# The first gate input loaded and scanned in two halves, and the early shares of the DMA engines in a planner set anew

## The chip, the cores and the metric

One core of a Trainium2 chip runs the kernel. The metric is device time in microseconds of one execution, as the median of several. The profile of one execution lists every instruction with its engine, its line, its start and what released it. The engines are TensorE (PE; its weight loads are listed as PEld), VectorE (DVE), ScalarE (ACT), GpSimd (POOL) and SyncE (SP). SP issues loads, stores and transposing transfers, POOL issues the weights' transfers, and 16 DMA engines move all of them.

## The reference

A gated linear attention over 4 batches, 8 heads, 768 steps and 48 channels, and behind it a gated feed-forward block over the 3072 tokens:

```python
f = 1.0 / (1.0 + np.exp(-f_logit))
for t in range(S):
    state = f[:, :, t, :, None] * state + np.einsum('bhd,bhe->bhde', k[:, :, t], v[:, :, t])
    y[:, :, t] = np.einsum('bhd,bhde->bhe', q[:, :, t], state)
x = np.ascontiguousarray(y.transpose(0, 2, 1, 3)).reshape(B * S, H * D)
gate = np.maximum(x @ w_gate, 0.0)      # 384 -> 1536
val = x @ w_val
out = (gate * val) @ w_out              # 1536 -> 384
```

## The kernel before, in words

**Tiling.** The sequence is cut into six chunks of 128 steps. The first four chunks are worked in pairs: a *unit* (d, b) is pair d (chunks 2d and 2d + 1) of batch b, so there are eight units; units (0, 0) to (0, 3) are called unit 0, 1, 2, 3 here. Chunks 4 and 5 are worked chunk by chunk (`attention_front`, `attention`). The 512 tokens of one chunk over four batches go through the feed-forward block together.

**One unit** (`attention_unit`). Four loads bring f, k, q and v (`load_unit`, 384 KB each, rows of 384 bytes). They are called f0, k0, q0, v0 for unit 0, and so on. ACT turns f into log gates (Exp at L587, Ln at L588, into `bneg`). PE sums them along the sequence with triangular matrices (the scan, L595 and L596: two PSUM banks, two products of 384 columns each). ACT takes exponentials of the sums (L600, L602) and of the totals (L626, into `decu`). POOL multiplies k by them (L604) and DVE multiplies q (L607), into `hats`. In pair 0, PE transposes the `hats` (L638) and DVE or ACT copies them to `qkT` (L646, L647); in later pairs a transposing transfer does it, issued by SP (L554, called a turn). PE multiplies q by k (scores, L677), DVE masks them into `ptm` (L682), POOL copies v into `vpad` (L613), PE forms the update of the state (L659), DVE and POOL update it (L569, L572, L574), and PE forms the outputs inside and across the halves (L708, L693). ACT or DVE copies them to `xT` (L724).

**Feed-forward.** For each of twelve blocks j of 128 hidden channels PE makes a gate bank and a value bank (L894, three products each, a *pass*), ACT takes the relu (L900) and DVE multiplies (L904, into `gT`). In the first group of 512 tokens, blocks 0 to 5 are done for two batches at a time (passes of 256 columns, twelve pairs of passes in all), blocks 6 to 11 for four at once (512 columns). Then PE multiplies `gT` by the output weights (L917), ACT copies (L927, into `osb`) and SP stores (L931).

**Weights.** POOL issues them in three parts each: wg0 and wv0 cover blocks 0 to 2, wg1 and wv1 blocks 3 to 5, wg2 and wv2 blocks 6 to 11, and wo0 to wo2 the output weights. Each waits for a load, as the list `first` says: `wg0@k0` is issued once k0 has landed, in POOL's queue between POOL's other work.

**What sets the order.** Every engine runs a fixed queue. A planner (class `Plan`) writes it when the kernel is built: a list schedule with a cost for each operation, in which the operation that can start first goes first, and due times of transfers from class `Rings`. `Rings` holds the loads' queue (`hw`) and the weights' queue (`sw`). While weights are moving, loads get a share of the engines and take longer by that much (`through`):

```python
SHARE, AHEAD, LAND = 0.16, 1500, 0.65
...
self.sw_free = begin + work / 0.87
```

The plan is made four times over, each time with the weights' stretches of the last. On the chip an operation waits for semaphores alone; due times decide only where it stands in its queue. Behind the plan, gaps of PE before 24 us are filled with products of zeros that keep PE active (`warm`, L976): so many as the planned gap divided by a cost for each.

**The first scan's place.** ACT's queue begins with Exp and Ln of f0, which wait for f0's landing; PE's queue has zeros before the first scan. POOL's queue has wg0's issue before the first k products.

Of the kernel before, what the change touches and what calls it, by code (L numbers as in the profile page):

```python
# [5 lines left out]
AF = mybir.ActivationFunctionType  # L6
# [38 lines left out]
class Rings:  # L45


    SHARE, AHEAD, LAND = 0.16, 1500, 0.65

    def __init__(self, busy):  # L50
        self.busy = busy
# [6 lines left out]
    def through(self, t, work):  # L58
        for a, b in self.busy:
            if b <= t:  # L60
                continue
            if t < a:
                if work <= a - t:
                    return t + work
                work -= a - t
                t = a
            if work <= (b - t) * self.SHARE:
                return t + work / self.SHARE
            work -= (b - t) * self.SHARE
            t = b  # L70
        return t + work

# [25 lines left out]

    def sw(self, at, work):
        begin = max(at, self.sw_free)  # L100
        self.sw_free = begin + work / 0.87
        self.made.append((begin, self.sw_free))
        return self.sw_free + self.LAND


class Plan:
# [9 lines left out]
    def add(self, eng, emit, reads=(), writes=(), occ=0.5, lat=0.2, prio=0, opens=(), after=(), follows=()):  # L116
        op = Op(eng, emit, list(reads), list(writes), occ, lat, prio, opens, after, follows)
        op.idx = len(self.ops)
        self.ops.append(op)
        return op  # L120
# [190 lines left out]
def bass_hgrn2_outer__then__ffn_reglu_kernel(  # L311
# [11 lines left out]
    pe_hats = {0}  # L323
    x_way = {4: "xbar", 5: "xbar"}
    flight = (4, 2)
    first = "f0 k0 q0 f1 v0 k1 q1 v1 wg0@k0 wv0@v0 wg1@k1 wv1@q1 f2 wg2@v1 wv2@wg1 k2 wo0@wv1 wo1@wg2 q2 v2 wo2@v2 f3 k3 q3 v3".split()
    B, H, S, D = q.shape
    C = 128
    NC = S // C
    HD = H * D  # L330
# [14 lines left out]
    bneg = sb("bneg", [128, NB, 2, H, 64], BF16)  # L345
# [30 lines left out]
    upto = sb("upto", [128, C], BF16)  # L376
    below = sb("below", [128, C], BF16)
# [10 lines left out]
    add = pl.add  # L388
    gp, ve, sc, te, sy = nc.gpsimd, nc.vector, nc.scalar, nc.tensor, nc.sync
# [5 lines left out]
    PE_L = 0.17  # L395

    def act_t(n):
        return dict(occ=max(0.1, n * 0.00097), lat=0.3)
# [55 lines left out]
    def dma(op, slot, flow, n=1, descs=0, ring="hw"):  # L454

        if slot not in slots:
            slots[slot] = [nc.alloc_semaphore(f"d_{slot}"), 0]
        slots[slot][1] += 16 * n
        op.sem, op.goal = slots[slot]
        op.flow, op.descs, op.ring = flow, descs, ring  # L460

    srcs = {"f": f_logit, "k": k, "q": q, "v": v}

    def slot_of(n, c, pr):
        return (2 * c + pr) % NL[n]

    def in_keys(n, c, b0, b1):
        return [f"{n}{slot_of(n, c, b // 2)}_{b % 2}" for b in range(b0, b1)]

    def load_unit(n, d, b, after=()):  # L470
        t = ld[n]
        row = NL[n] * 2 * HD
        c, pr = 2 * d + b // 2, b % 2
        src = bass.AP(tensor=srcs[n].tensor, offset=b * H * S * D + 2 * d * C * D, ap=[[2 * D, 128], [S * D, H], [1, 2 * D]])
        dst = bass.AP(tensor=t, offset=slot_of(n, c, pr) * 2 * HD, ap=[[row, 128], [2 * D, H], [1, 2 * D]])
        last = tails.get("load")
        op = add("SP", lambda: sy.dma_start(dst, src), [], in_keys(n, c, 2 * pr, 2 * pr + 2), occ=0.5, lat=1.13,
                 prio=d * 200 + b * 10, after=after, follows=[last] if last else [])
        tails["load"] = op
        dma(op, f"{n}{slot_of(n, c, pr)}", 1.79 if n == "f" and d + b == 0 else 1.215, 1, 1024)  # L480
        return op

    def load(n, c, b0, b1, after=()):
# [18 lines left out]
    def load_w(nm, s, after):  # L502
        j0, j1 = WB[nm][s:s + 2]
        if nm == "wo":
            src = bass.AP(tensor=w_out.tensor, offset=j0 * 128 * DM, ap=[[DM, 128], [128 * DM, j1 - j0], [1, DM]])
            dst = wo[:, j0:j1, :]
        else:
            src = bass.AP(tensor=wsrc[nm].tensor, offset=j0 * 128, ap=[[DFF, 128], [128 * DFF, NK], [1, (j1 - j0) * 128]])
            dst = (wg if nm == "wg" else wv)[:, :, j0 * 128:j1 * 128]
        last = tails.get("load_w")  # L510
        op = add("POOL", lambda: gp.dma_start(dst, src), [], [f"{nm}{s}"], occ=0.8, lat=2.05, prio=0 if nm != "wo" and s < 1 else 20, after=after,
                 follows=[last] if last else [])
        tails["load_w"] = op
        dma(op, f"{nm}{s}", 2.5 if nm == "wo" else 0.53 + 0.44 * (j1 - j0), ring="sw")
        return op

    loads, done = [], {}
    for item in first:
        item, _, behind = item.partition("@")
        need = [done[behind]] if behind else []  # L520
        if item[0] == "w":
            op = load_w(item[:2], int(item[2:]), need)
        else:
            op = load_unit(item[0], 0, int(item[1:]), need)
            loads.append(op)
        done[item] = op

    def chain(line, *args, **kw):

        last = tails.get(line)  # L530
        tails[line] = add(*args, follows=[last] if last else [], **kw)
        return tails[line]
# [44 lines left out]
    def attention_unit(d, b):  # L577
        w0 = 8 * d + 2 * b
        late = d > 0 or b > 1
        P = w0 * 10 if late else (0, 6)[b]  # L580
        c0, pr = 2 * d + b // 2, b % 2
        raw = {n: ld[n][:, slot_of(n, c0, pr), :, :, :].rearrange("p b h d -> p (b h d)") for n in "fkqv"}
        by_i = {n: raw[n].rearrange("p (h i d) -> p i h d", h=H, i=2) for n in "fkqv"}
        key = {n: in_keys(n, c0, 2 * pr, 2 * pr + 2) for n in "fkqv"}
        bi, e0, h0, q0, m0, v0, xi = w0 // 2 % NB, w0 % NE, w0 % NH, w0 % NQ, w0 % NM, w0 % NV, c0 % NX
        bn = bneg[:, bi, :, :, :]
        add("ACT", lambda: sc.activation(raw["f"], raw["f"], AF.Exp, scale=-1.0), key["f"], key["f"], prio=P, **act_t(2 * HD))  # L587
        add("ACT", lambda: sc.activation(bn[:, :, :, 0:D], by_i["f"], AF.Ln, bias=1.0), key["f"] + [f"bneg{bi}"],  # L588
            [f"bn{bi}_0", f"bn{bi}_1"], prio=P, **act_t(2 * HD))
        bkeys = ["upto", "below", f"bneg{bi}", f"bn{bi}_0", f"bn{bi}_1"]  # L590
        bc = [Bank("bc"), Bank("bc")]
        free = ["xT0_2"] if (d, b) == (0, 2) else []
        for i in range(2):
            def cum(i=i):
                te.matmul(bc[i].ap[:, 0:HD], upto[:, :], bn[:, 0, :, 0:D], start=True, stop=False)  # L595
                return te.matmul(bc[i].ap[:, 0:HD], (upto if i else below)[:, :], bn[:, 1, :, 0:D], start=False, stop=True)  # L596
            chain("cum", "PE", cum, bkeys + free, [bc[i]], occ=0.33, lat=PE_L, prio=P, opens=[bc[i]])
        for i in range(2):
            hi, ei = h0 + i, e0 + i
            add("ACT", lambda i=i, ei=ei: sc.activation(expo[:, ei, 1, :], bc[i].ap[:, 0:HD], AF.Exp, scale=1.0), [bc[i]],  # L600
# [29 lines left out]
        for x, part in ((1, (0,)), (0, (0, 1)), (1, (1,))) if d in pe_hats else ():  # L630
            tp = Bank("tp")
            n = len(part)

            def transposes(x=x, tp=tp, part=part):
                t16 = tp.ap[:, :].bitcast(BF16)
                for i in part:
# [6 lines left out]
                  prio=P + 3, opens=[tp])  # L643
            to = qkT[:, q0 + part[0]:q0 + part[-1] + 1, x, :, :].rearrange("p i n t -> p i (n t)")
            of = lambda tp=tp, n=n: tp.ap[:, 0:256 * n].bitcast(BF16).rearrange("p (i t) -> p i t", i=n)
# [8 lines left out]
        def state():  # L654
            for p in range(NP):
# [9 lines left out]
              kv, occ=0.45, lat=PE_L, prio=P + 4, opens=kv)  # L665
# [297 lines left out]
    for item in pend:  # L963
# [4 lines left out]
        prio=-30)  # L968
# [6 lines left out]
    def warm(n):  # L975
        return lambda: te.matmul(spare[:, 0:n], zeros[:, 0:128], zeros[:, 0:n], start=True, stop=True, skip_group_check=True)  # L976

    fillers, at, begun = {}, pl.free0["PE"], False
    for op in order["PE"]:
        gap, (n, each) = op.start - at, (64, 0.06) if at < 6.0 else (128, 0.054)  # L980
        if begun and op.start <= warm_until:
            fillers[op] = [warm(n)] * max(0, int((gap - 0.45) / each))
        begun = True
        at = op.start + op.occ
    sems = {e: nc.alloc_semaphore(f"e_{e}") for e in ("PE", "ACT", "DVE", "POOL")}
    for e in ("PE", "ACT", "DVE", "POOL"):
        n = 0
# [75 lines left out]
```

## Time and profile before

| what | value |
|---|---|
| three runs | 198.57, 200.08, 200.87 us (median 200.08) |
| the profiled execution | 200.2 us, span from its first to its last instruction 198.5 us |
| granted clock of PE | 0.999 |
| PE busy | 187.4 us, 94% of the span (zeros included) |
| ACT, DVE, POOL busy | 111.8, 103.8, 67.0 us |
| loads' and stores' queue | 28.58 MB, 65.3% of the 16 engines' span |
| weights' queue | 3.54 MB, 10.9% |
| chain that ended last | PE 69%, DMA 19%, ACT 4% |

The span is what the profile's rows add up to; the 1.7 us that the execution takes beyond it lie before the first and behind the last instruction. A row of the timeline gives start, busy time, engine, line, operation, output and input, count, and in brackets the idle time before it with what ended it. That releaser is inferred: where the named engine had long been done, it was another, often a transfer. A transfer's time to landing runs from its issue to its last byte.

### The profile page before, as it was taken

To read this page: it belongs to the slowest core of one execution; us is meant where nothing else is said; L and a number is where in the kernel's file an instruction comes from. 1 tells how busy PE (TensorE), PEld (TensorE's weight loads), DVE (VectorE), ACT (ScalarE), POOL (GpSimd) and SP (SyncE) were. 2 spreads that over 40 slices of the span, in tenths; PEclk is the share of its full clock that TensorE was granted. 3 is DMA by queue.
4 is the path that set the end of the run, shared out by engine and by line. 5 is a ranking of instruction groups with operands and counts; after the bars stand their busy time and mean duration, and the time that the engine had idled before them with its cause. 6 is when DMAs were issued, how large, how long until landed. Compare 5 with 4: busy or idle time off the path is not lost.

```text
span 198.5 us, 5453 instructions
## 1 busy us (share of the span) xinstructions
PE 187.4 (94%) x2298; PEld 108.8 (55%) x2298; DVE 103.8 (52%) x195; ACT 111.8 (56%) x234; POOL 67.0 (34%) x108
## 2 busy tenths in 40 slices
PE   7879798999999997999899998999999999999994
PEld 7657583566587643555455554555544555544552
DVE  5278554796679766855628522727433233443300
ACT  3768574576894896576845758343444334344311
POOL 8768450344671456367183440360000000000000
PEclk9999999999999999999999999999999999999999
DMA  6999999999999997999999898981321110111112
GB/s 165 304 257 261 242 208 209 247 269 261 282 234 217 262 259 147 174 223 173 200 216 184 180 204 123 224 163 54 89 69 40 40 39 3 40 40 43 40 71 88
DMA packets 93864, 32.46 MB, mean 164 GB/s; under 512 B 86928, under 2 KB 93840, under 8 KB 93840
## 3 DMA queue, kind: packets, MB, share of 16 engines
q1 hardware_dynamic: 89856, 28.58, 65.3%
q0 software_dynamic: 3984, 3.54, 10.9%
q8 instruction: 18, 0.29, 0.6%
q14 instruction: 6, 0.05, 0.1%
HBM read 25.95 MB, written 4.72 MB: 155 GB/s over the span
## 4 chain that ended last, share of the span: by engine, by line
PE 69%; DMA 19%; ACT 4%; SPq 2%; POOL 1%; issue 1%; DVE 1%
PE ps L894 37%; PE ps L917 21%; DMA qkT<-hats 7%; DMA wv<-in_moe_w_val_dram 5%; DMA wg<-in_moe_w_gate_dram 3%; DMA q_in<-in_q_dram 2%; DMA f_in<-in_f_logit_dram 2%; PE ps L810 1%; PE ps L708 1%; PE ps L677 1%; PE ps L659 1%; PE ps L595 1%; PE ps L596 1%; POOL hats L604 1%; SPq L554 1%
## 5 line engine op out<-in xcount | busy, mean ns | idle before, releaser
L904 DVE TENSOR_TENSOR gT<-relu,ps 128x512 bf16<-128x512 bf16 (+1 forms) x84 | 50.8, 610 | 59.6 <-PE ps L894 55.8
L900 ACT ACTIVATE relu<-ps 128x512 bf16<-128x512 f32 (+1 forms) x84 | 44.9, 537 | 32.8 <-PE ps L894 31.8
L894 PE MATMUL ps<-xT,wg 128*128 128x512 bf16 (+1 forms) x252 | 60.5, 349 | 1.1 <-DVE st L569 1.1
L894 PE MATMUL ps<-xT,wv 128*128 128x512 bf16 (+1 forms) x252 | 60.6, 349 | 0.7 <-DMA wv<-in_moe_w_val_dram 0.6
L917 PE MATMUL ps<-wo,gT 128*128 128x384 bf16 x288 | 51.9, 326 | 0.0
L917 PEld LDWEIGHTS ps<-wo,gT 128*128 128x128 bf16 x288 | 27.3, 98 | 19.0
L894 PEld LDWEIGHTS ps<-xT,wv 128*128 128x128 bf16 x252 | 23.1, 98 | 21.3 <-DMA wv<-in_moe_w_val_dram 1.4
L894 PEld LDWEIGHTS ps<-xT,wg 128*128 128x128 bf16 x252 | 23.5, 98 | 20.2 <-DVE st L569 1.3
L927 ACT ACTIVATE osb<-ps 128x384 f32<-128x384 f32 x24 | 11.8, 493 | 29.0 <-PE ps L917 28.8
L682 DVE TENSOR_TENSOR ptm<-ps,seen 128x512 bf16<-128x512 f32 x32 | 20.3, 683 | 5.3 <-PE ps L677 5.2
L604 POOL TENSOR_TENSOR hats<-k_in,expo 128x384 bf16<-128x384 f32 x16 | 15.7, 997 | 10.6 <-ACT expo L600 8.6
L770 POOL TENSOR_TENSOR hats<-k_in,expo 128x384 bf16<-128x384 f32 x8 | 7.9, 999 | 21.6 <-DMA k_in<-in_k_dram 15.2
L574 POOL TENSOR_TENSOR st<-ssum,decu 128x384 bf16<-128x384 f32 x12 | 10.0, 833 | 13.9 <-PE ps L708 8.0
L815 DVE TENSOR_TENSOR ptm<-ps,tri 128x512 bf16<-128x512 f32 x16 | 10.3, 685 | 7.4 <-PE ps L810 7.4
L572 DVE TENSOR_TENSOR ssum<-ps,st 128x384 f32<-128x384 f32 x16 | 8.8, 554 | 3.5 <-PE ps L659 1.9
L607 DVE TENSOR_TENSOR hats<-q_in,ps 128x384 bf16<-128x384 f32 x16 | 8.3, 549 | 3.6 <-ACT ps L602 3.6
L600 ACT ACTIVATE expo<-ps 128x384 f32<-128x384 f32 x16 | 7.1, 489 | 4.7 <-PE ps L596 4.7
L724 ACT ACTIVATE xT<-ps 128x384 bf16<-128x384 f32 x15 | 8.0, 597 | 2.6 <-PE ps L708 2.6
L613 POOL CAST vpad<-v_in 128x384 bf16<-128x384 f32 x16 | 7.8, 508 | 3.3 <-DMA v_in<-in_v_dram 3.3
L587 ACT ACTIVATE f_in<-f_in 128x768 f32<-128x768 f32 x8 | 6.7, 840 | 2.7 <-DMA f_in<-in_f_logit_dram 2.6
L773 POOL TENSOR_TENSOR hats<-q_in,expo 128x384 bf16<-128x384 f32 x8 | 7.8, 999 | 0.9 <-DMA q_in<-in_q_dram 0.9
L602 ACT ACTIVATE ps<-ps 128x384 f32<-128x384 f32 x16 | 7.3, 488 | 0.0
(81 smaller groups left out, 160.0 us busy)
## 6 DMA issues: line engine op xcount, KB each, us to landing
f_in<-in_f_logit_dram SPq DMA_DIRECT2D x12, 384.0 KB, 4.7
k_in<-in_k_dram SPq DMA_DIRECT2D x12, 384.0 KB, 6.1
q_in<-in_q_dram SPq DMA_DIRECT2D x12, 384.0 KB, 5.9
v_in<-in_v_dram SPq DMA_DIRECT2D x12, 384.0 KB, 5.8
out_dram<-osb SPq DMA_DIRECT2D x24, 192.0 KB, 1.9
wo<-in_moe_w_out_dram POOLq DMA_DIRECT2D x3, 384.0 KB, 9.1
wg<-in_moe_w_gate_dram POOLq DMA_DIRECT2D x2, 288.0 KB, 6.5
wv<-in_moe_w_val_dram POOLq DMA_DIRECT2D x2, 288.0 KB, 7.2
```

What stands on the lines that cost most here:

```text
L572: add("DVE", lambda: ve.tensor_tensor(tmp[:, :], kv.ap[:, 0:HD], s_old[:, :], ALU.add), [kv, f"S{b}_{(c + 1) % 2}"], [key], prio=P + 8, ** ...
L574: add("POOL", lambda: gp.tensor_tensor(t4(s_new), t4(tmp), rate, ALU.mult), [key] + dk, [f"S{b}_{c % 2}"], prio=P + 8, occ=0.79, lat=0.23)
L604: add("POOL", lambda i=i, hi=hi, ei=ei: gp.tensor_tensor(hats[:, hi, 1, :, 0:D], by_i["k"][:, i, :, :], expo[:, ei, 1, :].rearrange("p (h ...
L607: add("DVE", lambda i=i, hi=hi: ve.tensor_tensor(hats[:, hi, 0, :, 0:D], by_i["q"][:, i, :, :], bc[i].ap[:, 0:HD].rearrange("p (h d) -> p ...
L682: add("DVE", lambda i=i, j=j, s=sj[j]: ve.tensor_tensor(ptm_all[:, m0 + i, j, :, :], s.ap[:, :].rearrange("p (n t) -> p n t", n=NP), seen[ ...
L724: pl.either({"ACT": (lambda to=to, of=of: sc.activation(to, of(), AF.Copy), 0.372), "DVE": (lambda to=to, of=of: ve.tensor_copy(to, of()), ...
L815: add("DVE", lambda j=j, s=s: ve.tensor_tensor(ptm[mi][:, j, :, :], s.ap[:, :].rearrange("p (n t) -> p n t", n=NP), mask, ALU.mult), [s, " ...
L894: mm = te.matmul(bank.ap[:, 0:n], wt[:, kt, j * 128:(j + 1) * 128], xT[xi][:, b0:b1, kt, :], start=(kt == 0), stop=(kt == NK - 1))
L900: add("ACT", lambda: sc.activation(relu[ri][:, 0:n], gate.ap[:, 0:n], AF.Relu), [gate], [f"relu{ri}"], prio=P, **act_t(n))
L904: add("DVE", lambda: ve.tensor_tensor(gT[gi][:, j, n0:n1], relu[ri][:, 0:n], val.ap[:, 0:n], ALU.mult), [val, f"relu{ri}"], [f"gT{gi}_{j}_ ...
L917: mm = te.matmul(o[b].ap[:, 0:DM], gT[gi][:, j, b * C:(b + 1) * C], wo[:, j, :], start=(j == 0), stop=(j == NJ - 1))
L927: add("ACT", lambda b=b, oi=oi: sc.activation(osb[oi][:, :], o[b].ap[:, 0:DM], AF.Copy), [o[b]], [f"osb{oi}"], prio=P, **act_t(DM))
```

## The change

Three things change. First, f0 is loaded in two transfers, heads 0 to 3 and heads 4 to 7, which stand as `f0a f0b` at the head of `first`; `load_unit` takes a range of heads. For unit 0, Exp and Ln run on each half by itself, and the scan has eight products of 192 columns instead of four of 384: those of the first half of the heads can run before the second half has landed, and each bank is whole once both are done. Second, the planner's `Rings` now takes 0.5 instead of 0.16 as the loads' share while weights move, in stretches that begin before 17 us (`CALM`), and weights that begin before 17 us move at 0.6 instead of 0.87; later stretches are costed as before. Since due times decide the queues, the order of instructions on all engines changes from some 19 us on. Third, the cost of one product of zeros of 64 columns is put at 0.05 instead of 0.06 us, which changes how many fill a planned gap before 6 us.

```diff
-    SHARE, AHEAD, LAND = 0.16, 1500, 0.65
+    AHEAD, LAND, CALM = 1500, 0.65, 17.0
...
-            if work <= (b - t) * self.SHARE:
-                return t + work / self.SHARE
-            work -= (b - t) * self.SHARE
+            share = 0.5 if a < self.CALM else 0.16
+            if work <= (b - t) * share:
+                return t + work / share
+            work -= (b - t) * share
...
-        self.sw_free = begin + work / 0.87
+        self.sw_free = begin + work / (0.6 if begin < self.CALM else 0.87)
...
-    first = "f0 k0 q0 f1 v0 k1 q1 v1 wg0@k0 wv0@v0 wg1@k1 wv1@q1 f2 wg2@v1 wv2@wg1 k2 wo0@wv1 wo1@wg2 q2 v2 wo2@v2 f3 k3 q3 v3".split()
+    first = "f0a f0b k0 q0 f1 v0 k1 q1 v1 wg0@k0 wv0@v0 wg1@k1 wv1@q1 f2 wg2@v1 wv2@wg1 k2 wo0@wv1 wo1@wg2 q2 v2 wo2@v2 f3 k3 q3 v3".split()
...
-        dma(op, f"{n}{slot_of(n, c, pr)}", 1.79 if n == "f" and d + b == 0 else 1.215, 1, 1024)
+        dma(op, f"{n}{slot_of(n, c, pr)}" + ("" if nh == H else f"_{h0}"), (1.15 if h0 == 0 else 0.64) if nh < H else 1.215, 1, 128 * nh)
...
+        parts = ((0, 4), (4, H)) if d + b == 0 else ((0, H),)
+        for a, z in parts:
+            of = raw["f"][:, a * 2 * D:z * 2 * D]
+            add("ACT", lambda of=of: sc.activation(of, of, AF.Exp, scale=-1.0), fk(a, z), fk(a, z), prio=P, **act_t((z - a) * 2 * D))
+        for a, z in parts:
+            add("ACT", lambda a=a, z=z: sc.activation(bn[:, :, a:z, 0:D], by_i["f"][:, :, a:z, :], AF.Ln, bias=1.0),
+                fk(a, z) + [f"bneg{bi}"], bk(a, z), prio=P, **act_t((z - a) * 2 * D))
...
+        for n, (a, z) in enumerate(parts):
+            for i in range(2):
+                def cum(i=i, a=a, z=z, n=n):
+                    te.matmul(bc[i].ap[:, a * D:z * D], upto[:, :], bn[:, 0, a:z, 0:D], start=(n == 0), stop=False, skip_group_check=True)
+                    return te.matmul(bc[i].ap[:, a * D:z * D], (upto if i else below)[:, :], bn[:, 1, a:z, 0:D], start=False,
+                                     stop=(z == H), skip_group_check=True)
...
-        gap, (n, each) = op.start - at, (64, 0.06) if at < 6.0 else (128, 0.054)
+        gap, (n, each) = op.start - at, (64, 0.05) if at < 6.0 else (128, 0.054)
```

In the changed kernel, by its list of instructions, ACT's queue begins Exp, Ln of the first half, Exp, Ln of the second. PE's queue has 59 products of zeros before the first scan products (72 before). POOL's queue is the same up to wo0, then has both k products of unit 2 before wo1 (one of them stood behind it). SP's queue has the two halves first, then the same loads; further on, f and k of unit (1, 1) stand before the first stores and f of unit (1, 2) before the first turns.

More of the change, by code (lines that the diff above doesn't have):

```diff
@@ L468, in in_keys, with load_unit @@
         return [f"{n}{slot_of(n, c, b // 2)}_{b % 2}" for b in range(b0, b1)]
-    def load_unit(n, d, b, after=()):
+    def load_unit(n, d, b, after=(), heads=(0, H)):
         t = ld[n]
@@ L473, in load_unit @@
         c, pr = 2 * d + b // 2, b % 2
-        src = bass.AP(tensor=srcs[n].tensor, offset=b * H * S * D + 2 * d * C * D, ap=[[2 * D, 128], [S * D, H], [1, 2 * D]])
-        dst = bass.AP(tensor=t, offset=slot_of(n, c, pr) * 2 * HD, ap=[[row, 128], [2 * D, H], [1, 2 * D]])
+        h0, nh = heads[0], heads[1] - heads[0]
+        src = bass.AP(tensor=srcs[n].tensor, offset=(b * H + h0) * S * D + 2 * d * C * D,
+                      ap=[[2 * D, 128], [S * D, nh], [1, 2 * D]])
+        dst = bass.AP(tensor=t, offset=slot_of(n, c, pr) * 2 * HD + h0 * 2 * D, ap=[[row, 128], [2 * D, nh], [1, 2 * D]])
         last = tails.get("load")
-        op = add("SP", lambda: sy.dma_start(dst, src), [], in_keys(n, c, 2 * pr, 2 * pr + 2), occ=0.5, lat=1.13,
+        keys = in_keys(n, c, 2 * pr, 2 * pr + 2)
+        op = add("SP", lambda: sy.dma_start(dst, src), [], keys if nh == H else [keys[h0 // 4]], occ=0.5, lat=1.13,
                  prio=d * 200 + b * 10, after=after, follows=[last] if last else [])
         tails["load"] = op
-        dma(op, f"{n}{slot_of(n, c, pr)}", 1.79 if n == "f" and d + b == 0 else 1.215, 1, 1024)
+        dma(op, f"{n}{slot_of(n, c, pr)}" + ("" if nh == H else f"_{h0}"), (1.15 if h0 == 0 else 0.64) if nh < H else 1.215, 1, 128 * nh)
         return op
@@ L523, in bass_hgrn2_outer__then__ffn_reglu_kernel @@
         else:
-            op = load_unit(item[0], 0, int(item[1:]), need)
+            op = load_unit(item[0], 0, int(item[1]), need, {"": (0, H), "a": (0, 4), "b": (4, H)}[item[2:]])
             loads.append(op)
@@ L586, in attention_unit @@
         bn = bneg[:, bi, :, :, :]
-        add("ACT", lambda: sc.activation(raw["f"], raw["f"], AF.Exp, scale=-1.0), key["f"], key["f"], prio=P, **act_t(2 * HD))
-        add("ACT", lambda: sc.activation(bn[:, :, :, 0:D], by_i["f"], AF.Ln, bias=1.0), key["f"] + [f"bneg{bi}"],
-            [f"bn{bi}_0", f"bn{bi}_1"], prio=P, **act_t(2 * HD))
+        parts = ((0, 4), (4, H)) if d + b == 0 else ((0, H),)
+        fk = lambda a, z: key["f"] if z - a == H else [key["f"][a // 4]]
+        bk = lambda a, z: [f"bn{bi}_0", f"bn{bi}_1"] if z - a == H else [f"bn{bi}_{a // 4}"]
+        for a, z in parts:
[4 more added lines that the diff above has]
+                fk(a, z) + [f"bneg{bi}"], bk(a, z), prio=P, **act_t((z - a) * 2 * D))
         bkeys = ["upto", "below", f"bneg{bi}", f"bn{bi}_0", f"bn{bi}_1"]
@@ L592, in attention_unit @@
         free = ["xT0_2"] if (d, b) == (0, 2) else []
[L593 to L597, printed above, removed]
+        for n, (a, z) in enumerate(parts):
[4 more added lines that the diff above has]
+                                     stop=(z == H), skip_group_check=True)
+                chain("cum", "PE", cum, bkeys[:3] + bk(a, z) + free + ([bc[i]] if n else []), [bc[i]], occ=0.33 * (z - a) / H, lat=PE_L,
+                      prio=P, opens=[bc[i]] if n == 0 else [])
         for i in range(2):
```

## The prediction

> **What bounds the kernel now.** I read the 40 slices first, then the chain of waits, then the timeline of the first 32 us, then the DMA issues one by one, last the waits of TensorE (PE) behind 75 us.
>
> ```profile
> PE   7879798999999997999899998999999999999994
> DMA  6999999999999997999999898981321110111112
> ```
>
> PE is busy nearly everywhere, and to about 110 us the DMA engines are too. So the span (198.5 us) is PE's work plus PE's gaps, and before 100 us each gap has a transfer behind it. Windows of 5 us show no idle PE between 35 and 75 us: whatever PE loses or wins before 35 us is handed on whole to 75 us.
>
> ```profile
> 13.15 1.90 POOL hats L604 x2
> 15.05 5.97 DMA wg<-in_moe_w_gate_dram
> 21.03 0.29 issue
> 21.32 9.84 DMA wv<-in_moe_w_val_dram
> 31.16 0.05 issue
> 31.20 6.00 PE ps L894 x27
> ```
>
> These pieces of the chain (start, us, what) say that 15 to 31 us hangs on weights, not on the first scan. In the timeline:
>
> ```profile
> 4.35 0.84 ACT L587 ACTIVATE f_in<-f_in 128x768 f32<-128x768 f32 x1 [2.27 <-DMA f_in<-in_f_logit_dram]
> ...
> 5.22 0.84 ACT L588 ACTIVATE bneg<-f_in 128x768 bf16<-128x768 f32 x1
> ...
> 5.83 0.93 POOL L511 DMA_DIRECT2D wg<-in_moe_w_gate_dram  x1 [1.03 <-DMA k_in<-in_k_dram]
> ...
> 6.98 0.87 ACT L600 ACTIVATE expo<-ps 128x384 f32<-128x384 f32 x2 [0.92 <-PE ps L596]
> ...
> 13.15 1.95 POOL L604 TENSOR_TENSOR hats<-k_in,expo 128x384 bf16<-128x384 f32 x2 [1.92 <-ACT decu L626]
> ...
> 21.16 0.49 PE L894 MATMUL ps<-xT,wg 128*128 128x256 bf16 x3 [1.07 <-DVE st L569]
> ...
> 23.26 0.50 PE L894 MATMUL ps<-xT,wv 128*128 128x256 bf16 x3
> ...
> 31.20 0.82 PE L894 MATMUL ps<-xT,wv 128*128 128x512 bf16 x3 [0.59 <-DMA wv<-in_moe_w_val_dram]
> ```
>
> ACT (ScalarE) starts when f0 lands. The second pair of k products starts at 13.15, put down to ACT's decu, but k1 was the last to come: issued at 5.53, 7.5 us to landing, 13.0. The gate pass at 21.16 is put down to DVE, long done; wg1 landed then (issued 15.05, 6.0 us). 23.26 is wv1 (15.85 + 7.4), 31.20 is wv2 (21.32 + 9.8). The issues that the sum needs:
>
> ```profile
> k_in<-in_k_dram SPq DMA_DIRECT2D x1, 384.0 KB, 7.5
> ```
>
> ```profile
> q_in<-in_q_dram SPq DMA_DIRECT2D x1, 384.0 KB, 14.3
> ```
>
> ```profile
> q0 software_dynamic: 686, 1.03, 94.0%
> q1 hardware_dynamic: 555, 0.21, 20.2%
> ```
>
> The second is q2, issued at 14.76: it lands at 29.1. The last two are the stretch from 23 to 29 us (packets, MB, share): the weights' queue and the loads' queue. The loads get a sixth of the bytes.
>
> **The change part by part.** *f0 in halves.* Loads follow each other every 1.2 us (393 KB at the 323 GB/s that the windows show from 5 to 9 us), so the first half can land 0.6 us sooner, at 3.7; if both halves end together, at 4.33 as now. Exp and Ln of a half cost about 0.44 (L600: two of 384 in 0.87), so four take 1.75 against 1.72 now: two more instructions cost 0.05. Last Ln at 5.5 instead of 6.07; only two narrow products (192 columns) then stand before each exponential instead of two of 384. So ACT's expo starts near 6.0, not 6.98: 0.6 to 1.0 won on ACT. SP issues one DMA more (0.46 to 0.56), so k0 is issued 0.5 later; its bytes queue behind f0's anyway. PE's eight narrow products have the same columns as four wide ones.
>
> *Where that goes.* On POOL the first k products stand behind wg0's issue (5.83 + 0.93) and tri (to 7.08): of 0.9 some 0.5 is left. wv0's issue waits for v0 and starts at 9.46 in either. Then come the second k products, held by k1 at 13.0, and in PE's queue the first transposes of unit 1 stand before unit 0's intra products (L708, 14.63). k1's bytes come neither sooner nor later. So the front's gain ends there: 0 to 0.3 reaches the feed-forward passes, and the gates wg1 (21.05) and wv1 (23.25) hold them again. I take 0. The cover is the wait for k1; without it the change would be worth 0.5 to 0.9.
>
> *The plan's new shares.* They move no byte. They change the order that the planner writes: its belief in when loads land. By the planner's own due times q2 was to land at 33.0, later than the 29.1 of the trace; with the new shares it is due at 25.7, earlier. An in-order queue forgives the first error and not the second. Nothing that sets q2's real landing moves: POOL's queue up to wo0 is the same, and wg1, wv1, wg2, wv2 are held by k1, v1 and wg1.
>
> *The ledger of PE's queue, from the list of the changed kernel's instructions.* (a) Unit 1's intra products and unit 2's four scan products now stand before the wv1 pass; they fill the 1.07 at 20 to 21 us. Four products at 0.16 (23.92 to 24.57): 0.65 won at 23.26. (b) The twelve transposes of unit 2 (at 37.04 now) stand after the tenth of the twelve pairs of 256 columns. From 23.26 PE has thirteen passes at 0.327 (23.26 to 23.59) and four transposes (0.24), and arrives at 27.75. The transposes need unit 2's q products: q2 at 29.1 and two on DVE (1.01): 30.1. PE stands 2.35 us. (c) Then transposes 0.67, three passes to 31.75; scores wait for the copy on DVE, behind three gT products (3 x 0.39) and itself 0.69: 32.0; scores 0.57, one pass 0.33, one of 512 columns 0.65: the first wv2 pass at 33.5. wv2 has landed, so the 0.59 wait is gone. Before, the same work (31.20 plus 0.67 and 0.57) would be done at 32.44. Net loss 1.06. Bounds: were q2 there by 27, both waits vanish and 0.65 + 0.59 = 1.24 is won; if q2 comes 0.5 later the loss is 1.6. I take 1.06, because q2's row is this execution's own.
>
> The Trainium skill, "DMA: Bandwidth & Descriptors", section on queues, rings and completion order, says that each DMA engine takes turns between queue rows packet by packet, which speaks for an even share as the change assumes. The rows above agree by count (686 against 555) but not by bytes. With half of the time instead of 20.2%, q2's rest would pass in 2.4 us instead of 6 and land near 25.5; then the sum would be the one with 1.24 won, 198.6 instead of 200.9. The same page's rules for kernel authors advise to coalesce transfers, which speaks against the halves of f0; no row here shows a half load.
>
> *Queues behind.* While DVE holds q2's products, three gT products, the copy and four masks stand behind them; they cost PE nothing beyond (c), as its next passes find banks free. On POOL the k products of unit 2 move ahead of wo1's issue, which waits for wg2 (27.6) anyway: nothing.
>
> *45 to 65 us.* PE has no gap there now. In the new order the scan of unit (1,2) stands before the scores of (1,0), and four exponentials and two decay copies on ACT (4 x 0.44 + 0.36) stand before relus whose banks PE needs. Walking ACT and PE by their rows I find gaps of 0.35, 0.3 and 0.57 there. Bounds 0 (other slack takes them) and 1.2; I take 0.7.
>
> *After 75 us.* PE's waits there:
>
> ```profile
> 75.00:80.00 5.00, 3.94 (x60) 1.85 (x60) 3.62 (x7) 2.49 (x7) 2.86 (x4) 1.00 0.85 169
> ```
>
> ```profile
> PE ps L677 <- DMA qkT<-hats: 1.1, 1, 1.1
> PE ps L810 <- DMA qkT<-hats: 0.8, 1, 0.8
> ```
>
> 1.06 idle at 75 to 80 and 0.78 at 90 to 100, both for transposing transfers; 0.72 more at 120 to 125: 2.56 in all. SP's new order has f of unit (1,2) loaded before the first turns instead of after, 1.2 us less in front of the turns that PE waits for at 78, while PE comes 1.8 later. So the first wait goes: 1.06 back. The others hang on SP's later queue, where turns wait for products that PE's lateness delays: 0 back, bound 1.5.
>
> *Sum.* The profiled execution is 200.2 us (span 198.5 and 1.7 around it), 0.1 above the median of 200.08. 200.2 + 1.06 + 0.7 - 1.06 = 200.9; I say 201.0.
>
> **The rivals.** *Nothing is given back (slower).* Place: SP's queue. Stores wait for osb, turns for hats, loads for turns, and all of these for PE. If the turns of unit (1,0) (52.16 now) are issued over 1 us later, the loads and turns behind come as late as PE, and the 1.06 stays: 200.2 + 1.06 + 1.2 = 202.5, to 203.2 with a q2 that is later still. For it: SP waits 57.3 us in all for osb. Against it: the load taken ahead. *The late waits go (faster).* One load ahead of the turns lets all 2.56 of idle after 75 us close, and the gaps at 45 to 65 us don't come: 200.2 + 1.06 - 2.56 = 198.7; with the q2 stall half as long 197.5. Against it: those waits follow SP's later order, which hardly changes. *The change does not reach (same).* The stall at q2 is 1.3 instead of 2.35 and the rest cancels: 200.2.
>
> **How the numbers follow.** Forecast 201.0: 0.42, own range 199.9 to 202.0. Nothing given back: 0.32. Late waits go: 0.16. Same: 0.10. The range 198.8 to 203.2 reaches into both neighbours and leaves out 0.2. One per cent is 2.0 us, about what a measurement of this kernel can tell from no change (its three runs spread over 2.3). Below 198.1: most of the faster rival, 0.14. Above 202.1: most of the slower one and the edge of the forecast, 0.35. The rest, 0.51.
>
> **What would show it.** ACT's first expo near 6.0; second k products still at 13.1; PE idle for some 2.3 us before the twelve transposes, put down to DVE's hats; no wait for wv2; small PE gaps at 55 to 65; less than 0.5 idle at 75 to 80. Wrong if q2 lands before 28, if k1 lands well before 13, or if PE has no gap between 25 and 31 us.

## The result and the profile after

The changed kernel takes 201.71 us (median of 20 runs, 200.88 to 202.81), the kernel before 199.97 (20 runs). The ratio is 1.0108, 95% interval 1.0085 to 1.0131: slower by 1%. A later measurement gave 1.0114 (1.0073 to 1.0155). The forecast, 201.0, had the sign and put unit 2's wait where it came, but its loss of 0.8 us is under half of the measured one, which is 2.2 us (1.08% of 199.97). (The ratios leave out disturbed runs, so they are not quotients of the medians.)

The profiled execution of the changed kernel is the quickest of the 20: 200.88 us, span 199.2. Its slices, to be held against those of before (the first clock row is that of before, the rest is the changed kernel's):

```profile
PEclk9999999999999999999999999999999999999999
```

```profile
PE   7767997999999999999999999999999999999994
PEclk9997999999999999999999999999999999999999
DMA  5999999999999999989999798970221100111112
```

These things are new. The first DMA slice is a 5, not a 6: fewer bytes move in the first 5 us. The clock row has a 7 in the fourth slice (15 to 20 us), where PE ran at half speed for 3.4 us. And the 7 that PE had at 75 to 79 us is gone, with the 8s near 95 and 120 us. The chain of waits (start, us, what) now hangs on q2, not on the weights:

```profile
16.20 14.43 DMA q_in<-in_q_dram
...
31.12 0.56 DVE hats L620
31.68 0.05 issue
31.73 0.84 PE ps L651 x12
32.57 0.98 PE ps L907 x9
```

q2 is issued at 16.20, not 14.76, and lands at 30.63, not 29.05. The twelve transposes start at 31.73. The timeline, by engine:

```profile
3.41 0.52 ACT L596 ACTIVATE f_in<-f_in 128x384 f32<-128x384 f32 x1 [1.32 <-DMA f_in<-in_f_logit_dram]
...
6.05 0.87 ACT L613 ACTIVATE expo<-ps 128x384 f32<-128x384 f32 x2 [0.59 <-PE ps L607]
...
12.02 0.80 POOL L515 DMA_DIRECT2D wv<-in_moe_w_val_dram  x1 [1.96 <-DMA v_in<-in_v_dram]
...
15.04 1.95 POOL L617 TENSOR_TENSOR hats<-k_in,expo 128x384 bf16<-128x384 f32 x2 [1.25 <-DMA k_in<-in_k_dram]
...
16.08 0.40 PE L651 MATMUL ps<-ident,hats 128*128 128x128 bf16 x4 [1.64 <-POOL hats L617]
...
31.73 0.84 PE L651 MATMUL ps<-ident,hats 128*128 128x128 bf16 x12 [1.14 <-DVE hats L620]
...
35.04 0.81 PE L907 MATMUL ps<-xT,wv 128*128 128x512 bf16 x3
```

The first half of f0 lands at 3.39 (forecast 3.7) and expo starts at 6.05 (forecast near 6.0). But the second pair of k products starts at 15.04, not 13.15, and wv0's issue at 12.02, not 9.46, each held by a load (k1, v0) that came late. So PE is late before it reaches unit 2, stands 1.14 there, and makes the first wv2 pass at 35.04 where the ledger had 33.5. The first difference stands at the very front, in the packets moved between 3.5 and 5.0 us; first the kernel before, then the changed one:

```profile
DMA packets 1288, 0.48 MB, mean 323 GB/s; under 512 B 1288, under 2 KB 1288, under 8 KB 1288
```

```profile
DMA packets 881, 0.33 MB, mean 221 GB/s; under 512 B 881, under 2 KB 881, under 8 KB 881
```

A third of the packets is missing there, before any weight moves. The landings (us, when the last of the 16 engines has signalled, from each issue in the trace):

| kernel | k0 | v0 | k1 | wg1 | q2 | wv2 |
|---|---|---|---|---|---|---|
| before | 5.5 | 9.2 | 13.1 | 21.0 | 29.1 | 31.2 |
| changed | 6.6 | 11.7 | 15.0 | 23.0 | 30.6 | 32.6 |
| changed, second profile | 6.4 | 11.5 | 14.4 | 22.5 | 30.0 | 32.2 |

After 75 us the picture turns: the stretch from 75 to 80 us (columns as in the stretches of before: length, busy us of PE, PEld, DVE, ACT, POOL, clock, DMA share, GB/s) has no idle PE.

```profile
75.00:80.00 5.00, 5.00 (x73) 2.59 (x73) 3.58 (x7) 3.67 (x10) 2.86 (x4) 1.00 0.89 166
```

### The profile page after: what moved, and what is told of

Its sections match the earlier page's. It is cut to its first block, busy times and chain, and to the rows that moved or that the text cites. A ratio compares the mean times of both kernels' runs of the same rounds, so it can differ in the third digit from the quotient of the medians.

```text
span 199.2 us, 5450 instructions
## 1 busy us (share of the span) xinstructions
PE 189.2 (95%) x2293; PEld 110.8 (56%) x2293; DVE 104.7 (53%) x198; ACT 110.8 (56%) x233; POOL 66.9 (34%) x108
## 4 chain that ended last, share of the span: by engine, by line
PE 75%; DMA 10%; SPq 8%; ACT 4%; issue 1%; DVE 1%; DVEq 0%
PE ps L907 40%; PE ps L930 23%; SPq L481 7%; DMA q_in<-in_q_dram 7%; DMA f_in<-in_f_logit_dram 3%; PE ps L721 2%; PE ps L706 1%; PE ps L690 1%; ACT relu L913 1%; PE ps L823 1%; PE ps L672 1%; PE ps L761 1%; PE ps L651 1%; PE ps L860 1%; PE ps L606 1%
## 5 line engine op out<-in xcount | busy, mean ns | idle before, releaser
L907 PE MATMUL ps<-xT,wg 128*128 128x512 bf16 (+1 forms) x252 | 61.2, 352 | 0.2 <-DVE ptm L695 0.2
L930 PE MATMUL ps<-wo,gT 128*128 128x384 bf16 x288 | 51.2, 326 | 0.0
L907 PEld LDWEIGHTS ps<-xT,wg 128*128 128x128 bf16 x252 | 23.7, 99 | 19.5 <-DVE ptm L695 0.3
L651 PE MATMUL ps<-ident,hats 128*128 128x128 bf16 x64 | 5.6, 237 | 3.9 <-POOL hats L617 2.7
L737 ACT ACTIVATE xT<-ps 128x384 bf16<-128x384 f32 x12 | 6.8, 599 | 3.4 <-PE ps L721 3.2
L596 ACT ACTIVATE f_in<-f_in 128x768 f32<-128x768 f32 (+1 forms) x9 | 6.9, 765 | 2.5 <-DMA f_in<-in_f_logit_dram 2.5
```

What stands on the lines that cost most here:

```text
L907: mm = te.matmul(bank.ap[:, 0:n], wt[:, kt, j * 128:(j + 1) * 128], xT[xi][:, b0:b1, kt, :], start=(kt == 0), stop=(kt == NK - 1))
L930: mm = te.matmul(o[b].ap[:, 0:DM], gT[gi][:, j, b * C:(b + 1) * C], wo[:, j, :], start=(j == 0), stop=(j == NJ - 1))
```

## The experiments

Two theories stood against each other. *Supply*: the second transfer at the head of SP's queue makes k0 late, and everything behind it. *Order* (the prediction's): the new shares put unit 2's transposes where q2 has not landed, and the loads come as before. A summary first; "order" is the plan with the new shares and the scan by halves, "late" says whether k0's last engine (an expectation calls it the last ring) landed near 6.4 or at 5.5. The edits are shortened here to what they do; apart from them, the five edited kernels of this table keep the order of PE and ACT of the kernel that they are made from.

| kernel | order | late | ratio to before (95%) |
|---|---|---|---|
| changed, two series | new | yes | 1.0108 (1.0085-1.0131), 1.0114 (1.0073-1.0155) |
| changed, f0 in one transfer, two series | new | no | 1.0015 (0.997-1.006), 1.0040 (1.000-1.0079) |
| before, f0 in two transfers, two series | old | yes | 1.0027 (0.9986-1.0069), 1.0089 (1.005-1.0129) |
| before, k0 issued late | old | yes | 1.0066 (1.0025-1.0107) |
| before, tiny transfer ahead of k0 | old | yes | 1.0022 (0.9986-1.0057) |
| changed, f0 in one transfer, tiny one ahead of k0 | new | yes | 1.0131 (1.0077-1.0184) |

**Each part alone.** The kernel before with f0 in two transfers, nothing else:

```
-  dma_start(dst, src)                    # f0, heads 0..7
+  dma_start(dst_a, src_a); dma_start(dst_b, src_b)   # heads 0..3, 4..7; Exp waits for both
```

> The kernel before with its own order on every engine; only the first f is issued as two transfers (heads 0 to 3, heads 4 to 7), one after the other on SP, and the first Exp waits for both. Theory of the supply: the second issue costs the loads behind it a hole between 3.5 and 5 us, so k0 lands near 6.6 instead of 5.5, k1 near 14.5 to 15 instead of 13.1, q2 near 30.6 instead of 29.05, wv1 near 25 and wv2 near 32.6; PE waits in front of wg1 and wv2 grow together by 1 to 2 us, and the time is 200.8 to 202. Theory of the order: the two transfers carry the same bytes behind the same queue, k0 comes at most 0.5 later, k1 stays near 13.1, and the time is 200.0, within 0.3.

k0 landed at 6.47, k1 at 14.54, q2 at 30.2, wv2 at 32.2: late as in the changed kernel, in the old order. The time was 1.0027, less than the supply theory asked. It was measured again, beside the next one:

> The kernel before with the first f in two transfers, on the same chip. Theory: in the old order the late loads cost less, since PE's queue has no twelve transposes in front of what waits for q2: ratio 1.002 to 1.007. If late loads cost the same in any order, 1.008 to 1.012.

This time 1.0089; k0 at 6.18, k1 at 13.6. The two intervals touch (1.005 to 1.0069); by these two series the late loads cost the old order 0.3 to 0.9%.

The changed kernel with f0 in one transfer, everything else kept:

```
+  order["SP"].remove(f0b); f0b waits on f0a's transfer, which loads all eight heads
```

> The changed kernel with its own order on every engine and its scan by halves; only the first f comes in one transfer, which both halves wait for. Theory of the supply: k0 lands at 5.5 again, k1 near 13.1, q2 near 29; PE's wait for unit 2's q products is some 2.3 us, the feed-forward passes after it run 1.5 sooner than in the changed kernel, and since the waits after 75 us stay away the time is 199.8 to 200.5, 1.5 to 2 below the changed kernel. Theory of the order: what the change costs is the new place of unit 2's transposes, so the time stays at the changed kernel's 201.7 to 202.2; the first scan, which starts later by up to 0.6, costs nothing since k1 holds what follows.

1.0015, with an interval that lies below that of the changed kernel. The timeline shows the prediction's ledger with the loads on time:

```profile
27.44 0.49 PE L907 MATMUL ps<-xT,wv 128*128 128x256 bf16 x3
30.75 0.84 PE L651 MATMUL ps<-ident,hats 128*128 128x128 bf16 x12 [2.82 <-DVE hats L620]
...
34.06 0.81 PE L907 MATMUL ps<-xT,wv 128*128 128x512 bf16 x3
```

PE arrives at 27.44 + 0.33 = 27.77 (forecast 27.75) and waits 2.8 us for q2, which landed at 29.65. So the order theory's wait is real, and yet the kernel is hardly slower than before: what it loses at 30 us it gets back later, PE stands 0.41 between 75 and 140 us where the kernel before stood 2.56. Again, on the chip of the second series:

> The changed kernel with the first f in one transfer, on the same chip as the changed kernel. Theory: late loads are 1.0 to 1.8 us of the loss, and the order's own share is the rest: ratio 1.000 to 1.005. If the order alone were the cause, 1.008 to 1.013 as the changed kernel.

1.0040 beside 1.0114 of the changed kernel, whose repeat was

> The changed kernel as it is, beside the two that follow on one chip. k0 lands near 6.6 again, q2 over 30, and the ratio to before is 1.008 to 1.013.

**What makes k0 late.** Three edits of the kernel before. A tiny transfer between f0 and k0:

```
+  dma_start(spot[128 x 2 floats], f_logit[...])    # nothing reads it
   dma_start(k0)
```

> The kernel before; between the first f (one transfer) and the first k, SP issues a tiny transfer of 128 x 8 bytes whose result nothing reads, so that k0 is issued 0.5 us later behind one more transfer while f's own transfer is whole. If k0 is late in the changed kernel because it is issued 0.5 later as the third transfer, its last ring lands near 6.5 here too, k1 near 14.5, and the time is 0.5 to 1.5 above before. If it is late because halves of 512 packets feed the queue worse than a whole, k0 lands at 5.5 to 5.6, k1 near 13.1, and the time is that of before.

k0 at 6.38, k1 at 14.1, with f0 whole: the halves are not needed to make k0 late. The time, 1.0022, can't be told from no change. Then no further transfer at all, only a wait of SP in front of k0:

```
+  SP waits for DVE's memset of upto, then
   dma_start(k0)
```

> The kernel before with its own order and transfers; only the issue of the first k waits for DVE's memset of upto, which ends near 1.8, so that k0 is issued near 1.9 instead of 1.32 as the second transfer. If it is the later issue that opens the hole, k0's last ring lands near 6.4 to 6.6 and k1 near 14.5 as with two loads, time 0.2 to 1 over before. If it is the further transfer in the queue, k0 lands at 5.5, k1 near 13.1 and the time is that of before within 0.3.

The issue of k0 in the kernel before and in the changed one, and then that kernel's timeline, SP first and then POOL (start, us, engine, line, operation, what the engine waited for):

```profile
1.32 0.56 SPq L477 DMA_DIRECT2D k_in<-in_k_dram  x1
```

```profile
1.86 0.50 SPq L481 DMA_DIRECT2D k_in<-in_k_dram  x1
```

```profile
1.82 0.38 SPq L477 DMA_DIRECT2D k_in<-in_k_dram  x1
...
14.62 1.95 POOL L604 TENSOR_TENSOR hats<-k_in,expo 128x384 bf16<-128x384 f32 x2 [1.51 <-DMA k_in<-in_k_dram]
```

Issued at 1.82 instead of 1.32, k0's last engine landed at 6.37 instead of 5.53, k1 at 14.54, and the second k products started 1.47 later: time 1.0066. Half a microsecond at the issue became 0.84 at k0 and 1.5 at k1. In this kernel 2416 packets moved from 3.5 to 6.5 us, in the one with two loads 1982, in the kernel before 2564: the split opens the wider hole on average, but a load counts as landed when the slowest engine is through, and that engine is as late in all. Last, k0 split instead of f0:

> The kernel before; the first f is whole and the first k comes in two transfers instead. If splitting costs a fixed hole wherever it stands, f0 lands at 4.3, k0 at 5.5, q0 near 7.8 instead of 6.7 and k1 near 14.5, and the time is 0.5 to 1.5 above before. If the hole comes only where the queue is still empty, that is behind the first transfer, q0 lands at 6.7, k1 near 13.1, and the time is 200.0 to 200.5.

k0 at 5.85, q0 at 7.1, k1 at 13.4, ratio 1.0064 (1.0022 to 1.0106): half as late, and neither line of the expectation held. By SP's issues q0 was pushed from 1.94 to 2.47, and it landed 0.4 late. To close the circle, the changed kernel with f0 whole and the tiny transfer ahead of k0:

> The changed kernel with the first f in one transfer, and the tiny transfer of 128 x 8 bytes (its result is not read) between f0 and k0: the order of the changed kernel, loads late, but no split of f. If the lateness of the loads is all that the two transfers cost, k0 lands near 6.5, k1 near 14 to 15, q2 near 30, PE's wait for unit 2 grows to 3 or 4 us and the time is that of the changed kernel, 201 to 202. If the cost of the two transfers is in ACT or PE (halves that come apart), the time is that of the same order with one load, 200.0 to 200.4.

k0 at 6.55, q2 at 30.0, ratio 1.0131: with the loads late for another reason, f0's halves are not needed to lose what the changed kernel loses. (It has four runs, and each of them holds a stretch at half clock.)

**The second half on another queue.** The changed kernel, f0b issued by ACT at 0.83 while SP goes on with k0 at 1.33:

> The changed kernel with its own order; the second half of the first f is issued by ACT on its own queue, so that SP issues k0 at 1.3 again, right behind the first half. If the hole comes from SP's issue, k0 lands near 5.5 and all loads behind it come 1 to 1.5 sooner than in the changed kernel: time 199.8 to 200.6, that of the same order with one load. If two queues share the engines worse than one, f0's halves both land near 4.5 to 5, expo starts at 7 and k0 at 6: time 201 to 202.

> The changed kernel with the second half of the first f issued by ACT on its own queue, once more and with more runs; in its four runs k0 landed at 5.5 and q2 at 29.0, and two runs were 199.2 and 199.8, two 206.3 and 206.9. Theory of the supply: 199.3 to 200.3 in the undisturbed runs, 1.5 to 2 under the changed kernel. If the second queue brings its own disturbance, several runs lie above 203 again.

k0 landed at 5.5 both times. The first four runs lay at 199.2, 199.8, 206.3 and 206.9 and gave no ratio; the second series gave 1.0061 (1.0024 to 1.0098), with eleven of its twelve runs above the 199.3 to 200.3 expected, eight of them with a stretch at half clock. So the loads come on time, and about half of the loss stays. Nothing is gained in front either: f0a came at 3.9 and 4.0, not 3.4, and expo started at 6.4 and 6.6.

**The shares without the halves, and the halves without the shares.**

> The kernel before with the plan's new shares alone: the first f in one transfer, its scan whole, the order replanned. Theory of the order: unit 2's transposes again stand before the wv2 pass, q2 lands near 29, PE waits some 2.3 us for its products and no longer for wv2; the loss at the first wv2 pass is near 1.1, of which the waits after 75 us give back 1 to 2.2: 199 to 200.4 by the supply's theory, and 201 to 202 by the theory that the order alone is what the change costs. The granted clock of PE stays at full speed, since k1 comes at 13.1.

> The changed kernel with the plan's old shares: the first f in two transfers and its scan by halves, the order replanned with the shares of before. Theory of the supply: k0 lands near 6.6, k1 near 15, q2 near 30.6, wv2 near 32.6; unit 2's transposes stand late, so PE waits for wg1 and wv2 instead, 1.5 to 2 us more than in the kernel before, and the time is 201 to 202. Theory of the order: k1 near 13.1 holds the second k products whatever the first scan does, nothing is won or lost: 200.0, within 0.4.

The new shares with f0 and its scan whole: 1.0110 (1.0038 to 1.0182), with the loads on time (k0 5.5, k1 12.7). That is a miss for the supply theory. PE waited 2.69 for unit 2, as in the changed kernel with one load, but each of the four runs had one or two stretches at half clock. The stretches of the profiled one show both (the clock is the number behind the five engines, 0.66 and 0.76):

```profile
15.00:20.00 5.00, 4.81 (x69) 3.59 (x70) 2.61 (x6) 3.94 (x7) 3.81 (x6) 0.66 1.12 237
...
30.00:35.00 5.00, 3.76 (x57) 2.87 (x58) 4.37 (x10) 0.98 (x2) 0.00 (x0) 0.76 1.25 212
```

The old shares with f0 and its scan in halves: 1.0128 (1.0062 to 1.0195), k0 at 6.8, with new gaps of PE at 45 to 50 and 75 to 80 us (1.38 and 1.07 idle), since the plan reorders everything. Both are other orders, not the changed one less a part; they say that an order can lose 1% for its own reasons, and nothing finer. The third part of the change, the cost of a product of zeros, was not run by itself.

**The clock.** The changed kernel with zeros on PE in front of the two places where it waits for v0 and k1:

```
+  fillers: 12 zero passes before unit 0's state product, 24 before unit 1's first transposes
```

> The changed kernel with 12 and 24 more passes of zeros (about 0.65 and 1.3 us of PE) in front of unit 0's state product and unit 1's first transposes, where PE waits 0.8 and 1.6 us. In the changed kernel's profile the 3.4 us window with these waits has PE busy 0.52 of the time, and the window behind it gets half the clock. Theory of the clock: with the waits filled the window is busy over 0.7, the clock stays full in 15 to 25 us, and the time falls by some 0.5, which is what a run with such a window costs more than one without among the changed kernel's own runs (201.3, 201.8 and 202.4 for none, one and two): 201.0 to 201.4. Rival: the half clock is not set by how busy PE is; it stays, and the time is 201.7 or more by what the zeros delay.

Its stretches from 15 to 25 us, clock 1.00 and then 0.72:

```profile
15.00:20.00 5.00, 4.42 (x138) 3.38 (x135) 3.14 (x7) 3.00 (x6) 4.98 (x8) 1.00 1.20 261
20.00:25.00 5.00, 4.01 (x117) 2.78 (x117) 3.63 (x8) 2.49 (x4) 1.38 (x3) 0.72 1.24 233
```

The clock stayed full behind the filled wait, as the theory of the clock said, but a gap of 1.47 us in the middle of the scores of unit 1 (19.5 to 21.0, in which PE waited for nothing that the profile shows) was followed by half clock at 22.2 to 25.6. Ratio 1.0136 (1.0064 to 1.0209, four runs): no gain. In this one profile, filling one gap moved the slow stretch; whether zeros in all gaps would pay was not tried.

**Two attempts at a version that beats both.** Both have f0 in one transfer and tell the plan more of the truth: shares fitted to the landings (0.4 up to 17 us, 0.2 later; weights 0.6 and 0.8), or only that unit 2's q products start at 29.4.

> The changed kernel with the first f in one transfer, and shares in the plan that fit the landings seen (0.4 of the engines for loads beside weights up to 17 us, 0.2 later; weights at 0.6 and 0.8): q2 due at 30.3 where 29.1 to 29.7 were seen, wv2 at 30.3 where 30.4 to 31.2 were seen. The plan puts unit 2's twelve transposes behind the first wv2 passes. Theory of the order: PE's wait of 2.3 to 2.8 us for unit 2's q products shrinks to under 0.5 and a wait of 0.5 to 1 for wv2 comes in its place: time 198.5 to 199.8, below both kernels. Rival: what is won in front of 35 us is lost at the turns after 75 us as in the kernel before: 200.0 to 200.5.

> The changed kernel with one transfer for f, its new shares kept, but the plan is told that unit 2's q products start at 29.4 at the earliest; so only what hangs on q2 is placed later (the twelve transposes at 31.0 instead of 26.9 in the plan, behind seven more passes). Theory of the order: PE's wait of 2.8 us for these products goes down to under 0.5, a wait for wv2 of up to 0.6 comes instead, the late waits stay away: 198.5 to 199.5, 1 us under both. Rival: since stores, loads and turns are ordered anew too, what is won in front comes back as waits after 50 us: 200.0 to 200.6.

The first: 0.9996 (0.9964 to 1.0027), 199.38 median of 12, and not one run with half clock. It beats the changed kernel, and can't be told from the kernel before. In its profile (its slowest run) the wait for unit 2's q products is gone, and 0.51 us for wv2 stands in its place. The second moved the wait in the same way, as PE's timeline shows:

```profile
31.75 0.82 PE L908 MATMUL ps<-xT,wv 128*128 128x512 bf16 x3 [1.23 <-DMA wv<-in_moe_w_val_dram]
...
33.05 0.83 PE L652 MATMUL ps<-ident,hats 128*128 128x128 bf16 x12
```

The transposes wait for nothing and wv2 holds PE for 1.23 instead. The ratio, 1.0062 (0.9996 to 1.0128), decides nothing: its ten runs lie between 199.5 and 205.1, and why they scatter so was not found.

## Why the prediction was right in its sign and wrong in its size

*The step that failed* is in the part on f0 in halves: "k0 is issued 0.5 later; its bytes queue behind f0's anyway", and with it "Nothing that sets q2's real landing moves". The reasoning was that f0's bytes keep the engines busy to 4.3, and k0's issue at 1.9 is well ahead of that. The run that issues k0 at 1.82 and changes no transfer and no order refutes it: k0 comes 0.84 late, k1 1.5, and the kernel is 0.66% slower. So k1's bytes did come later, wv0 was issued at 12.02 and not "at 9.46 in either", and the front ledger missed a term of its own: late loads. It measured 1.0 at the first wv2 pass (35.04 in the changed kernel, 34.06 in the same order with f0 in one transfer), and q2 landed at 30.63 and 29.65. The planner holds the same belief: in `hw` a load begins at its issue plus 1.13 us or when the load before it ends, whichever is later, so an issue at 1.8 instead of 1.3 costs it nothing.

*What each part cost.* In runs with the clock at full speed throughout, which leave the clock's share out, the means are 199.43 (before, 56 runs), 200.04 (new order with one load, 14), 200.37 (old order with late loads, 12 runs of three kernels) and 201.27 (changed, 5): 0.6 for the order, 0.9 for the late loads, 1.8 for both. These runs come from several series; held against the runs of before in their own series, the order costs 0.5 and the late loads 1.0. The medians of all runs of these four groups say much the same: 200.02, 200.41, 201.08 and 201.71. With late loads the clock also falls more often. Counted over all runs, 42 of 102 of the kernel before hold a stretch at half clock, 8 of 22 of the new order with one load, 30 of 42 of the old order with late loads and 21 of 26 of the changed kernel; so part of what the late loads cost is paid through the clock.

*The order's own sum came near, in part by luck.* Forecast +0.8 (201.0 against 200.2); with the loads on time the two series give +0.3 and +0.8. But its parts were sized differently. The front loss, 1.06 forecast, was 34.06 - 32.44 = 1.6 with one load, since q2 landed at 29.65 there and not at 29.1 (the bound for a q2 half a microsecond later was 1.6), and 35.04 - 32.44 = 2.6 in the changed kernel. Of the gaps at 45 to 65 us (0.7 forecast) 0.25 came in the profile. After 75 us 1.06 was to come back, "the others" nothing: in the changed kernel's profile 2.25 came back (1.06 at 75 to 80, 0.78 at 90 to 100, 0.41 at 120 to 140). In the profile with one load the same sum is 1.6 + 0.33 - 2.15 = -0.2, and the spans differ by -0.1 (198.4 - 198.5): a front loss that was larger than forecast met a return that was larger too. In the changed kernel 2.6 + 0.25 - 2.25 = 0.6 is near the 0.7 by which the spans differ (199.2 - 198.5); that profile is the quickest run, the median lost 1.7.

The rival "nothing is given back" came nearer with its 202.5, but not by its mechanism, since the waits after 75 us did close.

*What was right.* expo at 6.05 and no gain from it, though two errors cancel there: the first half landed 0.3 sooner than forecast, and the four half instructions of ACT took 2.04 (3.41 to 5.45) and not 1.75; the PE gap before the twelve transposes, put down to DVE's hats (2.8 with one load, 1.1 in the changed kernel where PE comes late itself, 1.7 in its second profile); no idle at 75 to 80; the sign. What the prediction named as refuting it (q2 before 28, k1 well before 13, no gap between 25 and 31) did not come. The case that k1 would land *later* was not on the list. "Second k products still at 13.1" was the visible miss, 15.04. One reading was short: the DMA row has the engines busy to some 130 us, not 110; nothing in the sum hangs on it.

*The rule on shares.* The prediction weighed an even share of the engines and took the row, 20%. q2 took 14.4 us from issue to landing in the changed kernel too (14.3 before), and in no run of this order did it land near the 25.5 of an even share, so the row was the right choice for this order. (It is no constant: in the first of the two attempts, issued at 17.18 in another order, q2 took 9.1 us.)

*Splitting.* The Trainium skill, "Perfetto Trace Analysis", section on DMA optimizations, says that splitting a transfer may let some of it start sooner, and that the whole may be done sooner if the DMA engines are generally idle. The first shows here: f0's first half landed 0.93 sooner (3.39 against 4.32). The second's condition is not met: in a queue that is busy to some 130 us the other loads up to q2 landed 1.1 to 2.6 us later.

*Open.* Why a load issued at 1.8 to 1.9 instead of 1.32 reaches the slowest engine 0.6 to 1.2 late, although f0's bytes still move at 4.1; why the new shares with a whole scan (1.0110, four runs) lose more than with the halves (1.0015, 1.0040), with the loads on time in both.

## What to carry to other kernels

The front of a DMA queue is part of the critical path even where its waits don't show: before one adds an issue ahead of a long queue, delay the next issue by the same time in an experiment and look at the loads ten places behind. A load is as late as its slowest engine, so count landings, not mean bandwidth. And when an order's loss is forecast from one wait, try the order with the old transfers first: what it loses early it may get back late, and the transfers may be what is paid for.

## What the runs showed of the hardware

*Half clock after a half-empty window.* In the clock records of these profiles PE falls to half speed for exactly 3.41 us at a time, on a grid of 3.41 us whose start against the span differs from run to run. Of eleven such windows ahead of 40 us each followed a window in which PE was busy 0.29 to 0.68 of the time (union of the matmul records), with PE's waits of up to 2.7 us in them; behind windows over 0.7 there was none, while some windows of 0.48 to 0.69 were not punished. One window costs a run 0.009 of its mean clock, so it can be counted in each run: 28 of the 84 runs of the kernel before that the ratios use had at least one, 21 of 26 of the changed kernel, and within each the runs with one are 0.7 to 0.8 us longer (200.19 against 199.43, 201.98 against 201.27). The Trainium skill, "TensorE: Matmul & The Clock Gate", Part 1: The HAM clock gate, has the free-running window of 3413 ns and says that the clock falls after an idle window; here it fell after windows that were far from idle.

*An issue that waits costs more than its wait.* 0.5 us at the second issue of the program (1.82 against 1.32) was 0.84 at its own landing and 1.5 at the landing of the sixth load; 20 and 30 us later the weights behind it were still 1.5 and 1.2 late (wg1 22.6 against 21.0, wv2 32.3 against 31.2).
